# Counting the tokens of the last two batches on VectorE instead of TensorE in an attention and mixture-of-experts kernel

## The chip, the cores and the metric

The kernel runs on one core of a Trainium2 chip. The metric is the device time of one execution in microseconds. Five instruction engines work side by side: PE (TensorE, matrix products), ACT (ScalarE), DVE (VectorE), POOL (GpSimd) and SP (SyncE, which here only issues DMA transfers and loads registers). Each engine runs its own instructions in a fixed order, and semaphores tie the engines together.

## The reference

```python
# attention: u, v are (8, 2496, 256), z is (8, 2496, 64)
scores = (1 / S) * z @ z.T                 # per batch
attn   = maximum(scores, 0) ** 2           # no softmax
x      = u * (attn @ v)                    # 19968 tokens of 256
# mixture of experts: 8 experts, hidden width 1024, one expert for each token
logits = x @ w_gate + modality_bias[modality_id]
e_idx  = argmax(logits); gate = softmax(logits)[e_idx]
for e in range(8):                         # tokens of expert e
    out[mask] = gate * (maximum(x[mask] @ w1[e], 0) @ w2[e])
```

## The kernel before, in words

The first phase is attention, batch after batch. A batch is cut into five column chunks `c` of 512 queries (the last has 448), and a chunk into steps `i` of two key blocks of 128. A step makes scores `s` on PE, the root and the square on ACT (`r`), splits the square into a high part `ah` (L514, ACT mostly) and a low part `al` (L523, DVE), and PE adds three products (`ah` by `vh`, `ah` by `vl`, `al` by `vh`, L550) into four PSUM banks `acc`. Since the scores are symmetric, many squares are not computed again: DVE transposes them (`turn`, L413, L466), SP stores them in DRAM (`squares`, `corner`) and loads them for a later step (L402, L450).

When a chunk ends, ACT and DVE empty the banks into `x`, DVE multiplies by `ut` (L618), PE makes the logits (`pg`), and the chunk goes through DRAM (`rows`) into rows of one token. Then routing: `route_logits`, `route_exp`, `route_places` find the expert of each token and a running count within a partition; the counts over partitions and over earlier batches have to be added before each token's place in its expert's list is known (`route_slots`); `route_gates` makes the weight; `scatter` copies the two side columns into `x` (L802, DVE) and POOL scatters the rows into the experts' lists `xs` (L804). The kernel routes whole batches 0 to B-2; of the last batch, B-1, the first 8 columns (`SOON`) are routed before the phase ends, and the other 12 (`LATE`) within the second phase.

How the counts are added over partitions differs. For batches up to B-3, `route_sums` does it on DVE: four 32x32 transposes into `sums`, one scan over 128 values for each expert into `place`, four transposes back into `at`, one copy; at b == B-3 the total is spread over all partitions as `base` (one copy, four transposes). For the last two batches, `route_count` does it on PE: products with a triangular matrix `below` and a matrix `ones` into a bank `pc` (L746), and DVE adds them to `base` (L774, L776).

The second phase is the experts' network in tiles of 512 tokens. `choose` picks the expert with the most tokens; its first four tiles (t = -4 to -1, called EARLY) begin before the last tokens are routed. `plan` then lays out the rest; it is cut into eight parts, set between up-slices. A tile is eight up-slices (`up`: `ph` on PE, `hh` on ACT L1571, `hl` on DVE L1572) and two wide down-products (L1609). `put(slot, ...)` hangs other work behind an up-slice; slots 0 to 31 are the 32 up-slices of the tiles -4 to -1. `fetch_weights(t)` has SP load the expert's weights (`wr`, four transfers of 512 KB, L1018) after a register load from `meta`, the plan's result; ACT and DVE split them into `w` (L1033, L1038). `xg` are the tile's rows (L988), transposed into `xt` (L1065) and split into `xh`, `xl` (L1072, L1077). A tile's result goes over DRAM (`results`, L1625) back as `back` (L1628), is scaled by ACT (L1639) and scattered by POOL (L1648).

The order on every engine is written out by a planner for the first phase (a list of pieces, each with a time at which it is due) and by the order of the code for the second. Besides the diff's functions, the names that matter are `rest`, the planner's list of calls, and `between`, which `put` fills.

Of the kernel before, what the change touches and what calls it, by code (L numbers as in the profile page):

```python
# [8 lines left out]
F32 = mybir.dt.float32  # L9
F32R = mybir.dt.float32r  # L10
# [16 lines left out]
def tile_attention_moe(ctx: ExitStack, tc: tile.TileContext, ut, v, zt, mid, wg, mb, w1, w2, out):  # L27
# [71 lines left out]
    def bank_tile(shape, name):  # L99
        tag = bank["tag"]  # L100
        if isinstance(tag, list):
            tag.append(tag.pop(0))
            tag = tag[-1]
        return bank["pool"].tile(shape, F32, tag=tag, name=name)
# [9 lines left out]
    def iota_f32(shape, pattern, base, mult, name, pool=small):  # L114
        n = math.prod(shape[1:])
        i = raw.tile([P, n], I32, tag=name + "_i", name=name + "_i")
        f = pool.tile(shape, F32, name=name)
        nc.gpsimd.iota(i, pattern=pattern, base=base, channel_multiplier=mult)
        late.append((f, i))
        return f  # L120

    col = iota_f32([P, P], [[1, P]], 0, 0, "col", raw)
    part = iota_f32([P, 1], [[1, 1]], 0, 1, "part")
    em8 = iota_f32([P, E], [[1, E]], -E, 0, "em8")
    base0 = iota_f32([P, E], [[CAP, E]], -1, 0, "base0")
    begins = iota_f32([P, 1], [[0, 1]], -1, CAP, "begins")
    row_of = iota_f32([P, J], [[P, J]], 0, 1, "row_of")
    number = iota_f32([P, MAXT], [[1, MAXT]], -1, 0, "number")
    below = small.tile([P, P], F32R, name="below")
    ones = small.tile([P, P], F32R, name="ones")  # L130
    counts = small.tile([P, BLK], F32, name="counts")
    nc.vector.memset(counts, 0.0)
    sums = small.tile([BLK, P], F32, name="sums")
# [16 lines left out]
    def prep_constants(n):  # L150
        if n < 2:
            for f, i in late[n * 4:n * 4 + 4]:
                nc.vector.tensor_copy(out=f, in_=i)
            return
        nc.vector.tensor_scalar(out=below, in0=col, scalar1=part, scalar2=None, op0=ALU.is_gt)
        nc.vector.tensor_scalar(out=ones, in0=col, scalar1=0.0, scalar2=None, op0=ALU.is_ge)
        nc.vector.tensor_copy(out=place[0:E, 0:1], in_=begins[0:E])


# [549 lines left out]
    def route_places(b, cols):  # L709
        sh = RT[b]["sh"]  # L710
        shape = [P, cols.stop - cols.start, E]
        val = small.tile([P, NCOL, E], F32, tag="run", name="val")[:, 0:shape[1], :]
        em = em8.rearrange("p (o e) -> p o e", o=1).broadcast_to(shape)
        nc.vector.scalar_tensor_tensor(out=val, in0=sh, scalar=0.0, in1=em, op0=ALU.is_equal, op1=ALU.mult)
        idx = small.tile([P, NCOL, 1], F32, tag="idx", name="idx")[:, 0:shape[1], :]
        nc.vector.tensor_reduce(out=idx, in_=val, axis=AX.X, op=ALU.min)
        hot = small.tile([P, E, NCOL], F32, tag="hot", name="hot")
        if shape[1] < NCOL:
            nc.vector.memset(hot, 0.0)
        nc.vector.tensor_tensor(  # L720
            out=hot[:, :, cols].rearrange("p e j -> p j e"), in0=idx.broadcast_to(shape), in1=em, op=ALU.is_equal
        )
        if cols.stop == NCOL:
            nc.vector.memset(hot[LOW:P, :, NCOL - 2:NCOL], 0.0)
        run = small.tile([P, E, NCOL], F32, tag="run", name="run")
        nc.vector.tensor_tensor_scan(
            out=run.rearrange("p e j -> p (e j)"),
            data0=reset.rearrange("p e j -> p (e j)"),
            data1=hot.rearrange("p e j -> p (e j)"),
            initial=0.0,  # L730
            op0=ALU.mult,
            op1=ALU.add,
        )
        cnt = counts[:, 0:E] if b < B - 2 else small.tile([P, E], F32R, tag="cnt", name="cnt")
        nc.vector.tensor_copy(out=cnt, in_=run[:, :, NCOL - 1])
        RT[b].update(hot=hot, run=run, cnt=cnt)

    def route_count(b, cols):
        if b < B - 2:
            return  # L740
        cnt = RT[b]["cnt"]
        rows_of = (slice(0, P),) if cols == LATE else halves
        RT[b]["pt"] = [bank_tile([P, 2, E], "pc") for _ in rows_of]
        for n, lhs in enumerate((below, ones)):
            for pt, h in zip(RT[b]["pt"], rows_of):
                nc.tensor.matmul(out=pt[:, n, :], lhsT=lhs[h, :], rhs=cnt[h, :], start=True, stop=True)  # L746

    blocks = [slice(k * BLK, (k + 1) * BLK) for k in range(P // BLK)]

    def route_sums(b, at):  # L750

        for k in blocks:
            nc.vector.transpose(out=sums[:, k], in_=counts[k])
        nc.vector.tensor_tensor_scan(
            out=place[0:E, 1:P + 1], data0=ones[0:E].bitcast(F32), data1=sums[0:E], initial=place[0:E, 0:1],
            op0=ALU.mult, op1=ALU.add,
        )
        for k in blocks:
            nc.vector.transpose(out=at[k, :, 0], in_=place[:, k])
        nc.vector.tensor_copy(out=place[0:E, 0:1], in_=place[0:E, P:P + 1])  # L760
        if b == B - 3:
            nc.vector.tensor_copy(out=total[0:E], in_=place[0:E, 0:1].broadcast_to([E, BLK]))
            for k in blocks:
                nc.vector.transpose(out=base[k], in_=total)

    def route_slots(b, cols):
        run, hot = (RT[b][k] for k in ("run", "hot"))
        at = small.tile([P, BLK, 1], F32, tag="at", name="at")
        now = base[:, 0:E]
        if b < B - 2:  # L770
            route_sums(b, at)
        else:
            for n, x in enumerate(RT[b]["pt"]):
                nc.vector.tensor_tensor(out=at[:, 0:E, 0], in0=x[:, 0, :], in1=at[:, 0:E, 0] if n else now, op=ALU.add)  # L774
            for x in RT[b]["pt"]:
                nc.vector.tensor_tensor(out=now, in0=x[:, 1, :], in1=now, op=ALU.add)  # L776
        nc.vector.tensor_tensor(out=run, in0=run, in1=at[:, 0:E].broadcast_to([P, E, NCOL]), op=ALU.add)
        nc.vector.tensor_tensor(out=run, in0=run, in1=hot, op=ALU.mult)
        slot = small.tile([P, NCOL, 1], F32, tag="slot", name="slot")
        nc.vector.tensor_reduce(out=slot, in_=run.rearrange("p e j -> p j e"), axis=AX.X, op=ALU.add)  # L780
        sloti = small.tile([P, NCOL], I32, tag="sloti", bufs=2, name="sloti")
        nc.vector.tensor_copy(out=sloti, in_=slot[:, :, 0])
        RT[b]["sloti"] = sloti
# [36 lines left out]
    def t8(name, *shape, dt=F32):  # L820

        return small.tile([P, *(shape or (E,))], dt, name=name)
# [2 lines left out]

    def choose():

        cnt = t8("c_cnt")
        nc.vector.tensor_tensor(out=cnt, in0=base[:, 0:E], in1=base0, op=ALU.subtract)
        one_of = t8("c_most", 4)  # L830
        most, who, at = one_of[:, 0:1], one_of[:, 1:2], one_of[:, 2:4]
        nc.vector.tensor_reduce(out=most, in_=cnt, axis=AX.X, op=ALU.max)
        val = t8("c_val")
        nc.vector.scalar_tensor_tensor(out=val, in0=cnt, scalar=most, in1=em8, op0=ALU.is_equal, op1=ALU.mult)
        nc.vector.tensor_reduce(out=who, in_=val, axis=AX.X, op=ALU.min)
        nc.vector.tensor_scalar(out=skip, in0=em8, scalar1=who, scalar2=float(EARLY * T), op0=ALU.is_equal, op1=ALU.mult)
        nc.vector.tensor_scalar(out=at[:, 0:1], in0=who, scalar1=float(E), scalar2=None, op0=ALU.add)
        nc.vector.tensor_scalar(out=at[:, 1:2], in0=at[:, 0:1], scalar1=float(CAP), scalar2=None, op0=ALU.mult)
        nc.vector.tensor_copy(out=first, in_=at[0:1])

    def plan():

        cnt = t8("p_cnt")
        nc.vector.tensor_tensor(out=cnt, in0=base[:, 0:E], in1=base0, op=ALU.subtract)
        nc.vector.tensor_tensor(out=cnt, in0=cnt, in1=skip, op=ALU.subtract)

        up, upi = t8("p_up", 3, E), t8("p_upi", 3, E, dt=I32)
# [9 lines left out]
        quarters, halves, tiles = (up[:, n] for n in range(3))  # L857
        yield
        end = t8("p_end")
        nc.vector.tensor_tensor_scan(out=end, data0=ones[:, 0:E].bitcast(F32), data1=tiles, initial=0.0, op0=ALU.mult, op1=ALU.add)  # L860
        of_expert = t8("p_of", 2, E)
        beg, fin = of_expert[:, 0], of_expert[:, 1]
        start = t8("p_start")
# [564 lines left out]
    with tc.manual_schedule(engines={ET.PE, ET.Activation, ET.DVE, ET.Pool, ET.SP}):  # L1428
# [109 lines left out]
        for n, g in enumerate((24, 27, 30)):  # L1538
            at = rest.index((low, g)) + 1
            rest[at:at] = [(prep_constants, n)]  # L1540
        for f, *args in opening + rest:
            f(*args)
        for h in reversed(range(KD)):
# [294 lines left out]
    put(4, lambda: turn_rows(*end, 0))  # L1838
    put(5, lambda: turn_rows(*end, 1), lambda: store_rows(*end), lambda: load_natural(*end), lambda: make_gates(end[0], (end,)))
    put(6, lambda: take_gates(end[0], (end,)))  # L1840
    for slot, pieces in ((8, (route_gates,)), (10, (route_count, route_slots))):
        put(slot, *(lambda p=p: p(B - 1, LATE) for p in pieces))
    for n, k in enumerate(range(LATE.start, NCOL)):
        put(10 + n * 5 // 6, lambda k=k: scatter(B - 1, k))
    planning = plan()
    for slot in (10,11,12,13,14,14,15,15):
        put(slot, lambda: next(planning, None))
    put(16, lambda: fetch_weights(0))
    put(20, lambda: prefetch(-1))

    ph2.enter_context(tc.manual_schedule(engines={ET.PE, ET.Activation, ET.DVE, ET.Pool, ET.SP}))
# [117 lines left out]
```

## Time and profile before

| what | value |
|---|---|
| three runs | 2080.91, 2082.29 (median), 2083.0 us |
| profiled execution | 2084.35 us, of which the span of the program's instructions is 2082.5 us |
| PE busy | 2072.2 us, all but 10.3 us of the span |
| DVE busy | 1575.8 us (76%) |
| ACT busy | 1329.9 us (64%) |
| POOL busy | 350.1 us (17%) |
| chain that ended last | PE 95%, DMA 2%, DVE 1% |
| granted TensorE clock | 0.9 or more in all 40 slices |

Busy means that the engine executes; the span begins with the first instruction and ends with the last. A row of the timeline gives the start in us from the span's beginning, the duration, the engine, the line of the kernel, and the tile that is written and those that are read; in brackets at its end stands the idle time of the engine just before, with what ended it. The first phase ends at about 1222 us.

### The profile page before, as it was taken

What the parts mean: (1) busy time and instruction counts of PE and PEld (TensorE: products, weight loads), DVE (VectorE), ACT (ScalarE), POOL (GpSimd) and SP (SyncE); (2) the same over time, 40 slices, a digit from 0 to 9 for tenths busy, and PEclk for the clock granted to TensorE, in tenths of its full rate; (3) what the DMA queues carried; (4) which work ended last, traced back from release to release, by engine and by line L of the source; (5) the groups of instructions that cost most, each with busy time, mean ns of one, the idle gap of its engine ahead of it and who ended that gap; (6) DMA issues with size and microseconds to landing.
All of it is one profiled execution on the core that took longest, in us unless ns stands there. A gap on an engine that the chain in (4) does not pass through costs nothing.

```text
span 2082.5 us, 42408 instructions
## 1 busy us (share of the span) xinstructions
PE 2072.2 (100%) x15276; PEld 1751.1 (84%) x15276; DVE 1575.8 (76%) x2489; ACT 1329.9 (64%) x1715; POOL 350.1 (17%) x344
## 2 busy tenths in 40 slices
PE   9999999999999999999999999999999999999998
PEld 7888888889898888888888888888888888888887
DVE  9979788888888887897898776666566666666665
ACT  8659768768678678688677643545545555545554
POOL 0000022031030021030041303111211112121122
PEclk9999999999999999999999999999999999999999
DMA  8988899999889988999989976777777777776764
GB/s 202 300 265 206 252 257 236 259 255 237 257 239 242 270 238 233 279 238 240 279 240 245 271 162 181 201 187 192 202 189 197 191 196 201 183 210 186 196 187 128
DMA packets 617165, 464.82 MB, mean 223 GB/s; under 512 B 335177, under 2 KB 544105, under 8 KB 616945
## 3 DMA queue, kind: packets, MB, share of 16 engines
q1 hardware_dynamic: 601744, 420.95, 75.6%
q0 software_dynamic: 15200, 41.07, 5.7%
q8 instruction: 121, 1.98, 0.4%
q14 instruction: 100, 0.81, 0.1%
HBM read 286.27 MB, written 175.63 MB: 222 GB/s over the span
## 4 chain that ended last, share of the span: by engine, by line
PE 95%; DMA 2%; DVE 1%; SPq 1%; issue 1%; ACT 0%; POOLq 0%; ACTq 0%; POOL 0%; another core or an unknown queue 0%; DVEq 0%
PE acc L550 46%; PE ph L1567 20%; PE pw L1609 20%; PE s L375 7%; PE pg L651 1%; DMA xs<-x,sloti 0%; DVE al L523 0%; DMA r<-corner 0%; DMA vr<-in_v_dram 0%; PE po L1585 0%; DMA wr<-in_moe_w_dram 0%; DMA r<-squares 0%; DMA squares<-turn 0%; SPq L635 0%; SPq L425 0%
## 5 line engine op out<-in xcount | busy, mean ns | idle before, releaser
L550 PE MATMUL acc<-ah,vh 64*128 64x512 f32 (+1 forms) x3120 | 448.9, 383 | 0.8 <-ACT ah L514 0.5
L523 DVE TENSOR_TENSOR al<-r,ah 128x1024 fp32r<-128x1024 f32 (+1 forms) x359 | 419.6, 1183 | 31.0 <-ACT ah L514 25.1
L550 PE MATMUL acc<-al,vh 64*128 64x512 f32 (+1 forms) x3120 | 438.8, 381 | 0.0
L550 PE MATMUL acc<-ah,vl 64*128 64x512 f32 (+1 forms) x3120 | 437.1, 381 | 0.0
L1572 DVE SCALAR_TENSOR_TENSOR hl<-ph,hh 128x512 fp32r<-128x512 f32 (+1 forms) x312 | 210.3, 686 | 282.6 <-ACT hh L1571 237.3
L1567 PE MATMUL ph<-xh,w 128*128 128x512 f32 (+1 forms) x1248 | 396.0, 388 | 0.6 <-ACT xh L1072 0.6
L514 ACT CAST ah<-r 128x1024 fp32r<-128x1024 f32 (+1 forms) x342 | 345.6, 1032 | 44.6 <-PE acc L550 27.9
L804 POOL DMA_INDIRECT xs<-x,sloti x160 | 192.0, 1200 | 955.2 <-DVE x L802 689.7
L550 PEld LDWEIGHTS acc<-ah,vh 64*128 64x128 f32 x3120 | 305.0, 184 | 53.3 <-issue 1.2
L550 PEld LDWEIGHTS acc<-al,vh 64*128 64x128 f32 x3120 | 308.5, 184 | 47.9
L550 PEld LDWEIGHTS acc<-ah,vl 64*128 64x128 f32 x3120 | 301.6, 184 | 49.6
L1571 ACT ACTIVATE hh<-ph 128x512 fp32r<-128x512 f32 (+1 forms) x312 | 180.0, 592 | 235.2 <-PE ph L1567 221.9
L394 ACT ACTIVATE r<-s 128x1024 f32<-128x1024 f32 (+2 forms) x205 | 207.9, 1015 | 167.0 <-PE s L375 159.6
L1609 PE MATMUL pw<-hh,w 128*128 128x512 f32 (+1 forms) x1216 | 286.7, 388 | 0.0
L1567 PEld LDWEIGHTS ph<-xh,w 128*128 128x128 f32 x1248 | 234.2, 188 | 48.2 <-ACT xh L1072 0.9
L1609 PEld LDWEIGHTS pw<-hh,w 128*128 128x128 f32 x1216 | 228.3, 188 | 46.2
L413 DVE STREAM_TRANSPOSE turn<-r 128x512 f32<-128x512 f32 x316 | 205.3, 689 | 70.5 <-ACT r L491 44.3
L1648 POOL DMA_INDIRECT out_dram<-back,ids x152 | 148.4, 977 | 649.4 <-ACT back L1639 623.8
L1567 PE MATMUL ph<-xl,w 128*128 128x512 f32 (+1 forms) x624 | 242.2, 388 | 0.8 <-DVE xl L1077 0.8
L491 ACT ACTIVATE r<-r 128x1024 f32<-128x1024 f32 (+2 forms) x204 | 215.1, 1057 | 4.9
L375 PE MATMUL s<-zm,zk 64*128 64x512 f32 (+3 forms) x1440 | 192.5, 368 | 0.0
L1038 DVE TENSOR_TENSOR w<-wr,w 128x1024 fp32r<-128x1024 f32 x148 | 174.7, 1221 | 8.6 <-ACT w L1033 8.6
(194 smaller groups left out, 1703.0 us busy)
## 6 DMA issues: line engine op xcount, KB each, us to landing
wr<-in_moe_w_dram SPq DMA_DIRECT2D x148, 512.0 KB
squares<-turn SPq DMA_DIRECT2D x570, 128.0 KB
r<-squares SPq DMA_DIRECT2D x96, 512.0 KB
r<-squares SPq DMA_DIRECT2D x62, 448.0 KB
ut<-in_ut_dram SPq DMA_DIRECT2D x40, 512.0 KB
rows<-turn SPq DMA_DIRECT2D x160, 128.0 KB
x<-rows SPq DMA_DIRECT2D x160, 128.0 KB
xg<-xs SPq DMA_DIRECT2D x152, 128.0 KB
```

The costliest lines, as they stand in the source:

```text
L375: nc.tensor.matmul(out=s[t][:, :n_of], lhsT=lhs, rhs=mv[halves[t], ql, q], start=n == 0, stop=n == 2)
L394: nc.scalar.activation(out=r[:, t, :w], in_=s[t][:, :w] if g < 2 else s[:, :, :w], func=AF.Relu, scale=INV)
L413: nc.vector.transpose(out=dst[:, n], in_=src[:, n])
L491: nc.scalar.square(out=a[:, t, :w], in_=r[:, t, :w])
L514: copy(out=split_out(g, ah), in_=split_view(g, st_a[g]))
L523: nc.vector.tensor_tensor(out=split_out(g, al), in0=split_view(g, a), in1=split_out(g, ah).bitcast(F32), op=ALU.subtract)
L550: nc.tensor.matmul(out=acc[b, c][r][dh][:, :w], lhsT=V[b, k // J][y][halves[r], k % J, dh * P:(dh + 1) * P], rhs=x[halves[r], k % 2, :w], ...
L804: nc.gpsimd.indirect_dma_start(out=xs, out_offset=bass.IndirectOffsetOnAxis(ap=RT[b]["sloti"][:n, k:k + 1], axis=0), in_=x[:n, j, :], in_o ...
L1567: nc.tensor.matmul(out=ph, lhsT=lhs, rhs=rhs[:, k, :], start=n == 0, stop=n == 3 * KD - 1)
L1571: nc.scalar.activation(out=hh, in_=ph, func=AF.Relu)
L1572: nc.vector.scalar_tensor_tensor(out=hl, in0=ph, scalar=0.0, in1=hh.bitcast(F32), op0=ALU.max, op1=ALU.subtract)
L1609: nc.tensor.matmul(out=PO[t][h], lhsT=w[:, f, q, h * P:(h + 1) * P], rhs=HID[t, f][part], start=f == 0 and not q and not part, stop=bool(p ...
```

## The change

All batches are counted on DVE. The matrices `below`, `col` and `part` go, and so do the products into `pc`; `ones` becomes a plain constant that POOL sets. `route_sums` serves every batch, and `route_slots` calls it, but for the last 12 columns, where it stands alone in an earlier slot. The total is no longer spread once for the batches up to B-3; `all_counts` does this in `choose` and once more in `plan`. In the planner's list, three calls move: `choose` to just before `route_logits` of the first columns of the last batch, `route_slots` of the last two batches to just before their `route_gates`. In the second phase `route_sums` joins slot 8, the plan's eight parts move from slots 10, 11, 12, 13, 14, 14, 15, 15 to 11, 12, 13, 14, 14, 15, 19, 20, and the loading of tile 0's weights moves from slot 16 to slot 20.

```diff
-    below = small.tile([P, P], F32R, name="below")
-    ones = small.tile([P, P], F32R, name="ones")
+    ones = small.tile([P, P], F32, name="ones")
+    nc.gpsimd.memset(ones, 1.0)
...
-    def route_count(b, cols):
-        if b < B - 2:
-            return
-        cnt = RT[b]["cnt"]
-        rows_of = (slice(0, P),) if cols == LATE else halves
-        RT[b]["pt"] = [bank_tile([P, 2, E], "pc") for _ in rows_of]
-        for n, lhs in enumerate((below, ones)):
-            for pt, h in zip(RT[b]["pt"], rows_of):
-                nc.tensor.matmul(out=pt[:, n, :], lhsT=lhs[h, :], rhs=cnt[h, :], start=True, stop=True)
...
-        if b == B - 3:
-            nc.vector.tensor_copy(out=total[0:E], in_=place[0:E, 0:1].broadcast_to([E, BLK]))
-            for k in blocks:
-                nc.vector.transpose(out=base[k], in_=total)
+
+    def all_counts(name):
+        nc.vector.tensor_copy(out=total[0:E], in_=place[0:E, 0:1].broadcast_to([E, BLK]))
+        for k in blocks:
+            nc.vector.transpose(out=base[k], in_=total)
+        cnt = t8(name)
+        nc.vector.tensor_tensor(out=cnt, in0=base[:, 0:E], in1=base0, op=ALU.subtract)
+        return cnt
...
     def route_slots(b, cols):
-        run, hot = (RT[b][k] for k in ("run", "hot"))
-        at = small.tile([P, BLK, 1], F32, tag="at", name="at")
-        now = base[:, 0:E]
-        if b < B - 2:
-            route_sums(b, at)
-        else:
-            for n, x in enumerate(RT[b]["pt"]):
-                nc.vector.tensor_tensor(out=at[:, 0:E, 0], in0=x[:, 0, :], in1=at[:, 0:E, 0] if n else now, op=ALU.add)
-            for x in RT[b]["pt"]:
-                nc.vector.tensor_tensor(out=now, in0=x[:, 1, :], in1=now, op=ALU.add)
+        if cols != LATE:
+            route_sums(b, cols)
+        run, hot, at = (RT[b][k] for k in ("run", "hot", "at"))
...
+        for x, y in (((route_slots, B - 1, SOON), (route_gates, B - 1, SOON)), ((route_slots, B - 2, WHOLE), (route_gates, B - 2, WHOLE)), ((choose,), (route_logits, B - 1, SOON))):
+            rest.remove(x)
+            rest.insert(rest.index(y), x)
...
-    for slot, pieces in ((8, (route_gates,)), (10, (route_count, route_slots))):
+    for slot, pieces in ((8, (route_gates, route_sums)), (10, (route_slots,))):
...
-    for slot in (10,11,12,13,14,14,15,15):
+    for slot in (11,12,13,14,14,15,19,20):
         put(slot, lambda: next(planning, None))
-    put(16, lambda: fetch_weights(0))
+    put(20, lambda: fetch_weights(0))
```

On PE, the count of batch B-2 stood between two half steps of the attention; `pc` is its bank, `below` and `ones` the two matrices. Before:

```order
1680 L550 MATMUL acc<-al,vh 128x512 x4
1681 L746 MATMUL pc<-cnt,below 128x8 x2
1682 L746 MATMUL pc<-cnt,ones 128x8 x2
1683 L550 MATMUL acc<-ah,vh 128x512 x4
1684 L550 MATMUL acc<-ah,vl 128x512 x4
```

The same place now:

```order
1674 L546 MATMUL acc<-ah,vh 128x512 x4
1675 L546 MATMUL acc<-ah,vl 128x512 x4
1676 L546 MATMUL acc<-al,vh 128x512 x4
1677 L371 MATMUL s<-zm,zk 128x512 x6
1678 L546 MATMUL acc<-ah,vh 128x512 x4
1679 L546 MATMUL acc<-ah,vl 128x512 x4
1680 L546 MATMUL acc<-al,vh 128x512 x4
1681 L546 MATMUL acc<-ah,vh 128x512 x4
1682 L546 MATMUL acc<-ah,vl 128x512 x4
```

The four small products are gone, and nothing else of PE's order has moved; the other two places (four products in batch B-1, two in the second phase) are alike.

On DVE, the end of the routing of the last batch's first columns, between the low parts `al` that PE needs. Before:

```order
1266 L523 TENSOR_TENSOR al<-r,ah 128x1024
1267 L413 STREAM_TRANSPOSE turn<-r 128x2x8x32 x2
1268 L774 TENSOR_TENSOR at<-pc,base 128x8
1269 L774 TENSOR_TENSOR at<-pc,at 128x8
1270 L776 TENSOR_TENSOR base<-pc,base 128x8 x2
1271 L777 TENSOR_TENSOR run<-run,at 128x160
1272 L778 TENSOR_TENSOR run<-run,hot 128x160
1273 L780 TENSOR_REDUCE slot<-run 128x20
1274 L782 CAST sloti<-slot 128x20
1275 L802 COPY x<-side 128x2
1276 L466 STREAM_TRANSPOSE turn<-r 128x2x4x32 x2
1277 L523 TENSOR_TENSOR al<-r,ah 128x1024 x2
```

The same place now:

```order
1264 L409 STREAM_TRANSPOSE turn<-r 128x2x8x32 x2
1265 L789 COPY x<-side 128x2
1266 L462 STREAM_TRANSPOSE turn<-r 128x2x4x32 x2
1267 L519 TENSOR_TENSOR al<-r,ah 128x1024 x2
1268 L789 COPY x<-side 128x2
1269 L743 STREAM_TRANSPOSE sums<-counts 32x32 x4
1270 L744 SCALAR_TENSOR_TENSOR place<-ones,place,sums 8x128
1271 L749 STREAM_TRANSPOSE at<-place 32x32 x4
1272 L750 COPY place<-place 8x1
1273 L764 TENSOR_TENSOR run<-run,at 128x160
1274 L765 TENSOR_TENSOR run<-run,hot 128x160
1275 L767 TENSOR_REDUCE slot<-run 128x20
```

The places of the tokens now come behind the corner's transpose and two `al`, and they take ten small instructions more, less the four from `pc`. The choice of the first expert, with its five instructions of `all_counts`, stands further up, before the logits of these columns.

On SP, tile 0's weights (`wr`) in the second phase; `meta` is the plan's result, `results_113` and `results_111` belong to the tiles -4 and -3. Before:

```order
705 L1625 DMA results_113<-yt 32x16x64 x4
706 L1628 DMA back<-results_113 128x4x256
707 L1005 TENSOR_LOAD meta
708 L1005 ISA x2
709 L1018 ISA
710 L1018 DMA wr<-in_moe_w_dram 128x1024
```

The same place now:

```order
705 L1613 DMA results_113<-yt 32x16x64 x4
706 L1616 DMA back<-results_113 128x4x256
707 L1613 DMA results_111<-yt 32x16x64 x4
708 L1616 DMA back<-results_111 128x4x256
709 L990 TENSOR_LOAD meta
710 L990 ISA x2
711 L1003 ISA
712 L1003 DMA wr<-in_moe_w_dram 128x1024
```

The weights' four transfers now stand behind the next tile's results and their way back. Earlier on SP, the first register load from `first` moves from between two loads of `corner` and `squares` in batch B-1 to behind 20 more transfers.

## Rows read from the trace of the kernel before

**Rows 1.** The page: busy us of the engines, share, instructions.

```profile
PE 2072.2 (100%) x15276; PEld 1751.1 (84%) x15276; DVE 1575.8 (76%) x2489; ACT 1329.9 (64%) x1715; POOL 350.1 (17%) x344
```

**Rows 2.** Waits of PE: line, releaser, us in total, times, longest.

```profile
PE ph L1567 <- DVE xl L1077: 0.8, 1, 0.8
PE ph L1567 <- ACT xh L1072: 0.6, 1, 0.6
PE acc L550 <- ACT ah L514: 0.5, 1, 0.5
```

**Rows 3.** Windows: stretch, its us, busy us (instructions) of PE, PEld, DVE, ACT, POOL.

```profile
1224.00:2000.00 776.00, 776.00 (x3455) 645.35 (x3454) 499.01 (x731) 382.05 (x596) 144.52 (x149) 1.00 0.73 192
```

**Rows 4.** Timeline of PE around the first `pc`.

```profile
1106.71 0.61 PE L550 MATMUL acc<-al,vh 64*128 64x512 f32 x4
1107.16 0.17 PE L746 MATMUL pc<-cnt,below 64*128 64x8 f32 x2
...
1108.77 0.86 PE L375 MATMUL s<-zm,zk 64*128 64x512 f32 x6
```

**Rows 5.** Timeline of PE around the second `pc`.

```profile
1160.39 0.17 PE L746 MATMUL pc<-cnt,below 64*128 64x8 f32 x2
...
1163.38 0.62 PE L550 MATMUL acc<-ah,vh 64*128 64x512 f32 x4
```

**Rows 6.** Timeline of PE around the third `pc`, in the second phase.

```profile
1244.53 0.39 PE L1567 MATMUL ph<-xh,w 128*128 128x512 f32 x1
...
1245.20 0.39 PE L1567 MATMUL ph<-xl,w 128*128 128x512 f32 x1
```

**Rows 7.** By tile `place`: instructions, ns min/median/max, first and last start, forms.

```profile
L759 DVE STREAM_TRANSPOSE at<-place x24: 199/202/206, 273.9 to 1024.5; 32x32 f32<-32x32 f32 x24
L754 DVE TENSOR_TENSOR_SCAN place<-ones,place,sums x6: 472/473/474, 273.4 to 1023.4; 8x128 f32<-8x128 f32 x6
```

**Rows 8.** By tile `base`, columns as in rows 7.

```profile
L776 DVE TENSOR_TENSOR base<-pc,base x5: 156/166/167, 1109.3 to 1249.3; 128x8 f32<-128x8 f32 x5
```

**Rows 9.** Timeline of DVE: the choice of the first expert, and a later idle time.

```profile
1118.79 0.12 DVE L829 TENSOR_TENSOR c_cnt<-base,base 128x8 f32<-128x8 f32 x1
...
1120.29 0.17 DVE L802 COPY x<-side 128x2 f32<-128x2 f32 x1
...
1137.56 0.69 DVE L611 TENSOR_TENSOR x<-acc,x 128x512 f32<-128x512 f32 x1 [2.23 <-ACT x L607]
```

**Rows 10.** Timeline of DVE from the last batch's first places on.

```profile
1163.26 0.12 DVE L774 TENSOR_TENSOR at<-pc,base 128x8 f32<-128x8 f32 x1
...
1165.12 0.16 DVE L802 COPY x<-side 128x2 f32<-128x2 f32 x1
...
1165.94 2.32 DVE L523 TENSOR_TENSOR al<-r,ah 128x1024 fp32r<-128x1024 f32 x2
...
1186.84 1.23 DVE L523 TENSOR_TENSOR al<-r,ah 128x1024 fp32r<-128x1024 f32 x1 [9.32 <-ACT ah L514]
```

**Rows 11.** Timeline of PE: a reader of these `al`; tile 0's first product.

```profile
1167.68 0.62 PE L550 MATMUL acc<-al,vh 64*128 64x512 f32 x4
...
1306.28 0.39 PE L1567 MATMUL ph<-xh,w 128*128 128x512 f32 x1
```

**Rows 12.** Chain of waits: start us, us, what; the last corner's way back.

```profile
1179.00 6.67 DMA r<-corner
```

**Rows 13.** By tile `first`, columns as in rows 7.

```profile
L975 SPq TENSOR_LOAD <-first x4: 267/370/492, 1145.1 to 1238.6; - x4
```

**Rows 14.** Timeline of SP, tile 0's weights and what follows.

```profile
1270.95 7.14 SPq L1018 DMA_DIRECT2D wr<-in_moe_w_dram  x4
...
1284.95 0.38 SPq L1628 DMA_DIRECT2D back<-results  x1
1286.25 1.92 SPq L988 DMA_DIRECT2D xg<-xs  x4
```

**Rows 15.** Timeline of DVE where tile 0's rows are transposed.

```profile
1299.56 1.24 DVE L1065 STREAM_TRANSPOSE xt<-xg 128x1024 f32<-128x1024 f32 x1
```

More of the change, by code (lines that the diff above doesn't have):

```diff
@@ L120, in iota_f32 @@
         return f
-    col = iota_f32([P, P], [[1, P]], 0, 0, "col", raw)
-    part = iota_f32([P, 1], [[1, 1]], 0, 1, "part")
     em8 = iota_f32([P, E], [[1, E]], -E, 0, "em8")
@@ L154, in prep_constants @@
             return
-        nc.vector.tensor_scalar(out=below, in0=col, scalar1=part, scalar2=None, op0=ALU.is_gt)
-        nc.vector.tensor_scalar(out=ones, in0=col, scalar1=0.0, scalar2=None, op0=ALU.is_ge)
         nc.vector.tensor_copy(out=place[0:E, 0:1], in_=begins[0:E])
@@ L733, in route_places, with route_count, route_sums @@
         )
-        cnt = counts[:, 0:E] if b < B - 2 else small.tile([P, E], F32R, tag="cnt", name="cnt")
-        nc.vector.tensor_copy(out=cnt, in_=run[:, :, NCOL - 1])
-        RT[b].update(hot=hot, run=run, cnt=cnt)
-    def route_count(b, cols):
-        if b < B - 2:
-            return
-        cnt = RT[b]["cnt"]
-        rows_of = (slice(0, P),) if cols == LATE else halves
-        RT[b]["pt"] = [bank_tile([P, 2, E], "pc") for _ in rows_of]
-        for n, lhs in enumerate((below, ones)):
-            for pt, h in zip(RT[b]["pt"], rows_of):
-                nc.tensor.matmul(out=pt[:, n, :], lhsT=lhs[h, :], rhs=cnt[h, :], start=True, stop=True)
+        nc.vector.tensor_copy(out=counts[:, 0:E], in_=run[:, :, NCOL - 1])
+        RT[b].update(hot=hot, run=run)
     blocks = [slice(k * BLK, (k + 1) * BLK) for k in range(P // BLK)]
-    def route_sums(b, at):
+    def route_count(*_):
+        return
+    def route_sums(b, cols):
+        at = RT[b]["at"] = small.tile([P, BLK, 1], F32, tag="at", name="at")
         for k in blocks:
@@ L754, in route_sums @@
         nc.vector.tensor_tensor_scan(
-            out=place[0:E, 1:P + 1], data0=ones[0:E].bitcast(F32), data1=sums[0:E], initial=place[0:E, 0:1],
+            out=place[0:E, 1:P + 1], data0=ones[0:E], data1=sums[0:E], initial=place[0:E, 0:1],
             op0=ALU.mult, op1=ALU.add,
@@ L826, in choose @@
     def choose():
-        cnt = t8("c_cnt")
-        nc.vector.tensor_tensor(out=cnt, in0=base[:, 0:E], in1=base0, op=ALU.subtract)
+        cnt = all_counts("c_cnt")
         one_of = t8("c_most", 4)
@@ L841, in plan @@
     def plan():
-        cnt = t8("p_cnt")
-        nc.vector.tensor_tensor(out=cnt, in0=base[:, 0:E], in1=base0, op=ALU.subtract)
+        cnt = all_counts("p_cnt")
         nc.vector.tensor_tensor(out=cnt, in0=cnt, in1=skip, op=ALU.subtract)
@@ L859, in plan @@
         end = t8("p_end")
-        nc.vector.tensor_tensor_scan(out=end, data0=ones[:, 0:E].bitcast(F32), data1=tiles, initial=0.0, op0=ALU.mult, op1=ALU.add)
+        nc.vector.tensor_tensor_scan(out=end, data0=ones[:, 0:E], data1=tiles, initial=0.0, op0=ALU.mult, op1=ALU.add)
         of_expert = t8("p_of", 2, E)
```

## The prediction

> **What bounds the kernel now.** I read the page's busy times first, then the waits of TensorE (PE), then windows, then the timelines at the places that the change touches. PE is busy 2072.2 us [rows 1] of a span of 2082.5 us, so all other engines together can hold back only 10.3 us. The waits of PE name what little of it lies inside: 0.8 and 0.6 us before the first up-products of the second phase, and once 0.5 us on an `ah` [rows 2]. From 1224 to 2000 us PE is busy 776.00 of 776.00 us [rows 3]. So a gain can come only from work taken off PE or from these waits, and a loss only from a delay that outlasts the slack of an engine that is not the bound. The reader is to see that DVE's and SP's work is free as long as PE finds its operands.
>
> The sum is made against the profiled execution, 2084.35 us, which stands 2.06 us above the median of the three runs, 2082.29 us. A last step brings it back to that median.
>
> **Part 1, taken off PE.** Ten small products with their weight loads go. At the first place PE needs 1.61 us from 1107.16 to 1108.77 for three groups of four products; a group takes 0.45 us, from 1106.71 to 1107.16 [rows 4]. Three would be 1.36 us, so the four `pc` products cost 0.25 us, far less than their durations added up, since they overlap with their neighbours. At the second place it is 2.99 us for six such groups, 1160.39 to 1163.38 [rows 5], against 2.72 us: 0.27 us. At the third there are 0.67 us between a first and a third up-product [rows 6]; two products over all 128 rows take what four over 64 rows take, 0.45 us, so 0.22 us goes. Sum on PE: 0.25 + 0.27 + 0.22 = 0.74 us, or 0.04% of the time. That is the most that the change takes directly.
>
> Not all is kept. The first two places lie ahead of the wait on `ah`. That wait does not follow PE: DVE stood idle 9.32 us for the same `ah` at 1186.84 [rows 10], and the chain of waits there runs over the last corner's way back from DRAM, 6.67 us from 1179.00 [rows 12]. If PE arrives 0.52 us sooner and the corner does not, PE waits 0.52 us longer. The second wait, at the phase change, ends a chain that goes on from there over scatters on POOL, another corner and the first weights; it does not follow PE either. The third place lies in the gapless stretch, and its 0.22 us stays.
>
> **Part 2, added to DVE.** One call of the sums is eight transposes at 0.20 us, a scan at 0.47 us [rows 7] and a copy; for this and the other small copies I take the 0.17 us of an add of eight elements [rows 8]. That makes 1.6 + 0.47 + 0.17 = 2.2 us. It comes three times, and replaces four, four and two small adds, about 0.17 us each. The total and `base` in `choose` and `plan` are a copy and four transposes, about 1.0 us each; one such group was there before, in batch B-3.
>
> In batch B-2 the sums and slots (3.6 us with the four operations on `run`) now stand directly before the gates. `choose`, 1.50 us from 1118.79 to 1120.29 [rows 9], goes away from there. Net, what follows is about 2.1 us late. DVE has idle time to take it up, 2.23 us in one piece at 1137.56 alone [rows 9]. In between every `al` could be late; PE would wait 2.1 us at the very most. I take nothing, since PE has no wait on an `al` anywhere in the list of before [rows 2], so DVE is ahead here by some amount.
>
> In the first columns of B-1, `choose` with its `base`, 1.50 + 1.0 = 2.5 us, comes in first; the slots, 1.86 us from 1163.26 to 1165.12 [rows 10], go behind two `al`. So the corner's transpose and these two `al` are 0.7 us late. The first of them, half of the 2.32 us from 1165.94, was ready at 1167.1 [rows 10], and PE reads it at 1167.68 [rows 11]. It would be ready at 1167.8, while PE, 0.5 us ahead, asks at 1167.2: PE waits about 0.6 us here, between 0 and 1. That eats the gain of the first two places, which is lost at the corner anyway. The sums and slots behind them make the rest up to 4.3 us late, against an idle time of 9.32 us on DVE [rows 10]. All of it fits, so nothing of this reaches the second phase unless the corner moves.
>
> In the second phase the sums (2.2 us) and the plan's `base` are in slots 8 to 11, in which DVE is about 2 us later with `hl`. The bank that a slot needs is that of four slots earlier, and the order leaves this distance as it was. I take nothing, at most 1 us.
>
> **Part 3, SP's order.** The register load from `first`, 0.27 to 0.49 us each [rows 13], leaves the stretch before the last corner, with its two register instructions perhaps 0.9 us. Everything on SP behind it could be that much sooner, the corner that ends PE's wait included; against that stands the corner's transpose, 0.7 us later on DVE, and a load of `ut` that waits for DVE's product, later by 4.3 us, ahead of the corner's load. Ends: 0.9 us sooner, 0.6 us later. I take 0.1 us sooner, since SP was issuing into full queues and a place freed there is not a transfer made faster.
>
> **Part 4, tile 0's weights.** Before, their four issues ran from 1270.95 for 7.14 us, and the rows `xg` were issued from 1286.25 [rows 14]. Now the weights follow a `back` which was issued at 1284.95 [rows 14]: weights from about 1285.4 to 1292.5, `xg` from about 1292.6 on, 6.3 us later than before, for 1.92 us [rows 14]. If the last of it takes as long as the corner, 6.67 us [rows 12], it lands at 1301.2; before it was used from 1299.56 [rows 15], and three steps of about 1.24 us (transpose, high, low) would end at 1304.9. PE's first product of tile 0 started at 1306.28 [rows 11]. It fits, with 1.4 us to spare. I take nothing; the other end is 3 us, if weights and rows queue behind each other for twice the corner's time or so.
>
> This is 2.5 MB within 10 us, hence a question of transfers. SBUF tiles on the left side now start 576 bytes lower. The Trainium skill ("DMA: Bandwidth & Descriptors", "How a descriptor splits into AXI transactions") says that a descriptor which does not start on a 256-byte boundary costs one more, partly unused transaction; for bulk tiles that start on such a boundary now and did not before, this would make transfers slightly cheaper, for token rows nothing. No row shows a transfer's alignment, and by rows 2 PE waits for DMA hardly at all, so by the rule as by the rows the sum stays.
>
> **Sum.** 2084.35 - 0.22 (third place) - 0.1 (corner) = 2084.0 us profiled, and less 2.06 us: 2082.0 us against the median of before. Within 0.2%, or 4.2 us, a measurement of this kernel cannot tell a change; the forecast is no change.
>
> **Rivals.**
> The first: everything is kept. SP's freed 0.9 us moves the corner and the chain behind it, so both waits shrink with PE's earlier arrival: -0.74 - 0.9 = -1.6 us, 2080.7 us. For it: the chain runs through SP several times [rows 12]. Against: `ut` and the transpose are later.
>
> The second is slower: tile 0's weights and rows come late, PE waits before its first up-product of tile 0, and nothing later gives it back, since PE is the bound. It decides from a landing of `xg` after about 1302.6 (1306.28 less three steps of 1.24 us). At a landing of 1306, nearly 5 us behind the slow landing above, the price is 3.4 us less the 0.3 gained: 2085.4 us. For it: 2 MB ahead of the rows in the same queues, and a `back` before them that had to wait for its results. Against: the four weights' issues took only 7.14 us with other transfers beside them [rows 14].
>
> The third: late low parts on DVE make PE wait where I take nothing: 2.1 us in batch B-2 and up to 1 us in the second phase. A wait ahead of the corner is taken back there up to 0.5 us, so +1.6 + 1 - 0.3: 2084.6 us at its worst.
>
> The fourth: the change doesn't do what it says: PE's small products were hidden in its pipeline, and leaving them out gives nothing: 2082.3 us, not to be told from the forecast.
>
> **How the numbers follow.** Forecast 0.66; rival 1 0.12; rival 2 0.10; rival 3 0.08; rival 4 0.04. The range reaches from below rival 1 to rival 2's price, 2079.8 to 2085.4 us, with a microsecond for the spread of the runs of before (2.1 us). Faster by over 0.2% needs 4.2 us, more than PE's work and all its inner waits (0.74 + 1.9 us) can give: 0.04. Slower by over 0.2% needs rival 2 at more than its price, or 2 and 3 together: 0.08. Same: 0.88.
>
> **What would show it.** Right: PE busy about 0.7 us less, no `pc`; PE's wait on `ah` near 1186 longer by about what is saved ahead of it; the rows of `xt` for tile 0 still ending before PE asks. Wrong: a wait of PE on `xl`, `xh` or `w` at about 1306 us; a wait on `al` over 1 us between 1110 and 1180; a phase change more than a microsecond earlier or later than before; a new wait on a `ph` bank between 1245 and 1280.

## The result and the profile after

The change made the kernel slower, by 13 us: 2094.77 us (median of 6, 2093.68 to 2096.96) against 2081.74 us (median of 6), a ratio of 1.0064 with a 95% interval of 1.0055 to 1.0074. The forecast was 2082.0 us, no change, and its range ended at 2085.4.

The page of the changed kernel, busy us as in [rows 1]:

```profile
PE 2083.7 (100%) x15266; PEld 1759.2 (84%) x15266; DVE 1583.8 (76%) x2510; ACT 1331.8 (64%) x1715; POOL 351.2 (17%) x343
```

PE executes ten products less and is busy 11.5 us more. The waits of PE, as in [rows 2]:

```profile
PE warm L1417 <- POOL zeros L110: 1.0, 1, 1.0
PE acc L546 <- DVE ah L494: 0.6, 1, 0.6
PE acc L546 <- DVE al L519: 0.5, 1, 0.5
```

The reader is to see what is not there: no wait in the second phase, none at the phase change. PE is not held back by anybody; it works more slowly. The stretch of [rows 3], after:

```profile
1224.00:2000.00 776.00, 776.00 (x3397) 635.18 (x3396) 497.07 (x733) 377.67 (x586) 145.08 (x148) 1.00 0.66 189
```

In the same 776 us, at the same granted clock of 1.00 (the 2.4 GHz level), PE starts 3397 products where it started 3455. (The last three numbers of such a row are the granted clock, the busy share of the DMA engines and the GB/s that they moved.) The timeline shows it product by product. Before, the first up-products of a tile:

```profile
1458.60 0.39 PE L1567 MATMUL ph<-xh,w 128*128 128x512 f32 x1
...
1459.73 0.61 PE L1567 MATMUL ph<-xh,w 128*128 128x512 f32 x2
```

After, the same five products of a tile that reads the weights W_0 (the tiles take W_0 and W_1 in turn):

```profile
1459.52 0.40 PE L1555 MATMUL ph<-xh,w 128*128 128x512 f32 x1
...
1460.69 0.63 PE L1555 MATMUL ph<-xh,w 128*128 128x512 f32 x2
```

And further on in a tile that reads W_1, three products:

```profile
1450.45 0.62 PE L1555 MATMUL ph<-xh,w 128*128 128x512 f32 x2
...
1451.13 0.62 PE L1555 MATMUL ph<-xh,w 128*128 128x512 f32 x2
```

From start to start that is 1.13 us for five before, 0.227 us each; 1.17 us, 0.234 each, with W_0; and 0.68 us for three, again 0.227, with W_1. From the starts of the products in the trace, 96 products (a tile's work) took 21.76 us before, in tile after tile. After, the tiles -4 to -1, which all read W_0, took 22.40 us, and later tiles 22.00 and 22.24 in turn. Over the 39 stretches of 96 products (`pc` left out of the count) it sums up to 855.9 us against 843.1, or 12.8 us, which is nearly all of the 13.0 lost. The 843.1 us hold the two waits of [rows 2] at the phase change, 0.8 and 0.6 us, which the changed kernel didn't have; the pace alone costs a little more, as e3 below shows.

What has W_0 to do with the change? Nothing reads or writes it differently, but tiles lie elsewhere. `below` (512 bytes a partition), `part` and `cnt` (32 each) are gone from the left side of SBUF, and every tile stacked behind them starts 576 bytes lower: `xh`, `xl`, `hh`, `hl`, W_1, and the attention's `vh`, `vl`, `ah`, `al`. 576 is 2 x 256 + 64. Before, all of these started 64 bytes past a multiple of 256; now they start at one. W_0 lies on the right side, in a pool opened after the constants' pool is closed. It stayed, 64 bytes past. These places are worked out from the program, for no trace shows an address; the experiments below test them. So weights and moving operand of one product lie alike (modulo 256) with W_1 and no longer with W_0.

### The profile page after: what moved, and what is told of

It reads as the page before. It is cut to its first block, busy times and chain, and to the rows that moved or that the text cites. A ratio compares the mean times of both kernels' runs of the same rounds, so it can differ in the third digit from the quotient of the medians.

```text
span 2092.9 us, 42408 instructions
## 1 busy us (share of the span) xinstructions
PE 2083.7 (100%) x15266; PEld 1759.2 (84%) x15266; DVE 1583.8 (76%) x2510; ACT 1331.8 (64%) x1715; POOL 351.2 (17%) x343
## 4 chain that ended last, share of the span: by engine, by line
PE 98%; issue 1%; ACT 0%; DMA 0%; DVE 0%; SPq 0%; POOLq 0%; POOL 0%; another core or an unknown queue 0%; DVEq 0%
PE acc L546 49%; PE ph L1555 21%; PE pw L1597 20%; PE s L371 7%; PE pg L647 1%; DMA squares<-turn 0%; PE warm L1417 0%; PE ph L1703 0%; ACT w L1018 0%; ACT r L390 0%; ACT back L1627 0%; DVE y L1674 0%; ACT part L1669 0%; SPq L421 0%; POOLq L1953 0%
## 5 line engine op out<-in xcount | busy, mean ns | idle before, releaser
L1555 PE MATMUL ph<-xh,w 128*128 128x512 f32 (+1 forms) x1248 | 400.5, 392 | 0.0
L1597 PE MATMUL pw<-hh,w 128*128 128x512 f32 (+1 forms) x1216 | 291.4, 392 | 0.0
```

Source lines behind the costliest of these rows:

```text
L1555: nc.tensor.matmul(out=ph, lhsT=lhs, rhs=rhs[:, k, :], start=n == 0, stop=n == 3 * KD - 1)
L1597: nc.tensor.matmul(out=PO[t][h], lhsT=w[:, f, q, h * P:(h + 1) * P], rhs=HID[t, f][part], start=f == 0 and not q and not part, stop=bool(p ...
```

## The experiments

The experiments move tiles by changing the size of unused tiles called `room`, of which the kernel has four; the second number of each diff line is in floats of 4 bytes. They ran in four groups on different chips, each beside the kernel before, whose own time there was 2079.27, 2080.68, 2081.59 and 2082.54 us; so times are compared within a group. Rows are the stretch from 1400 to 2000 us, columns as in [rows 3]: what counts is the number of products behind PE's 600.00 us. For the first two kernels it is, before and after:

```profile
1400.00:2000.00 600.00, 600.00 (x2666) 500.03 (x2665) 381.40 (x503) 304.88 (x472) 105.27 (x109) 1.00 0.73 194
```
```profile
1400.00:2000.00 600.00, 600.00 (x2625) 492.75 (x2624) 379.31 (x498) 302.07 (x464) 105.22 (x108) 1.00 0.66 190
```

**e1_after_left64**, the changed kernel with the left side where it was:

```diff
-    small.tile([P, 16], F32, name="room")
+    small.tile([P, 160], F32, name="room")
```

> The changed kernel with an unused tile made 576 bytes larger, so that every tile on the left side of SBUF (xh, xl, hh, hl, the weights W_1 of odd-even turn, and the attention's tiles) begins where it did before the change, 64 bytes past a multiple of 256, as the weights W_0 on the right side do in both kernels. Nothing else differs from the changed kernel. Theory A (places: PE's products in the second phase slow down when weights and moving operand begin at different offsets within 256 bytes): every up- and down-product is back at 0.227 us, a tile at 21.76 us instead of 22.00 and 22.24, PE busy about 2071 us, and as the phase change stays 3.4 us earlier than before, the time is 2078.5 to 2080 us. Rival B (order: the later work on DVE and SP slows PE): stays at 2094 to 2096 us.

Measured: 2079.90 us against 2079.27 (ratio 1.0007, 0.9998 to 1.0016).

```profile
1400.00:2000.00 600.00, 600.00 (x2666) 500.03 (x2665) 381.30 (x505) 306.14 (x474) 107.43 (x111) 1.00 0.72 195
```

The loss is gone with all of the change in order and counting left in. The gain of 3 us that I read from the phase change isn't there: see e9 and the next section.

**e2_before_left0**, the kernel before with its left side 64 bytes lower and nothing else:

```diff
-    small.tile([P, 16], F32, name="room")
```

> The kernel before with its first unused tile of 64 bytes left out, so that all tiles on the left side begin 64 bytes lower, at multiples of 256, while W_0 on the right side stays 64 past one; the order on every engine is that of the kernel before. Theory A: the products that read W_0 slow down, tiles -4 to -1 take about 22.4 us and of the others every second half-weighted 22.00 and 22.24 us, in all about 39 tiles x 0.36 = +13 us, 2095 to 2096 us. Rival B: unchanged, 2082 us.

Measured: 2092.61 us against 2079.27 (1.0065, 1.0049 to 1.0080); tiles of 22.40, then 22.00 and 22.24 us.

```profile
1400.00:2000.00 600.00, 600.00 (x2625) 492.75 (x2624) 378.96 (x498) 301.98 (x465) 104.97 (x108) 1.00 0.67 190
```

The whole loss without any of the change. Rival B, the order, is out.

**e3_after_w0at0**, the changed kernel with W_0 moved to a multiple of 256 too (W_0 is on the right side, where a larger `room` puts it lower):

```diff
-        pool.tile([P, 40], F32, name="room")
+        pool.tile([P, 56], F32, name="room")
```

> The changed kernel with an unused tile above W_0 64 bytes larger, so that W_0 on the right side too begins at a multiple of 256, as all on the left side does after the change. Theory A (weights and moving operand must lie alike, whatever the common offset): 21.76 us a tile, 2078.5 to 2080 us. Theory A' (the offset 64 itself is the good one): W_0's products stay slow or all get slow, 2094 us or more. Rival B: 2094 us.

Measured: 2078.36 us against 2079.27 (0.9997, 0.9988 to 1.0007), every full tile 21.76 us.

```profile
1400.00:2000.00 600.00, 600.00 (x2665) 499.87 (x2664) 379.88 (x502) 305.56 (x472) 109.15 (x112) 1.00 0.67 195
```

It is not the offset 64 that is good, but that weights and moving operand share one. The 39 stretches of 96 products take 841.7 us here; the changed kernel, with the same order and, like e3, no wait in the second phase, took 855.9, so the pace alone costs 14.2 us.

**e4_before_w0at0**, the same edit made to the kernel before, so that W_0 is at 0 and the left side at 64:

> The kernel before with W_0 at a multiple of 256 and everything on the left 64 past one: the difference of the changed kernel, with its sign turned. Theory A with a difference that counts either way: products with W_0 slow, about 2095 us. If only a moving operand below the weights' offset costs: 2082 us. Rival B: 2082 us.

Measured: 2082.16 us (one run; before 2079.27).

```profile
1400.00:2000.00 600.00, 600.00 (x2652) 497.79 (x2652) 378.56 (x500) 303.96 (x469) 106.19 (x109) 1.00 0.70 193
```

Neither expectation holds: tiles -3 and -2 take 21.97 us, 0.21 over 21.76 and so a third of what such a tile loses in e2. The difference counts both ways, but not equally.

**e5_after_w0at128, e6_after_w0at192, e11_after_w0at32**: the changed kernel (left side at 0) with the `room` of e3, 40 floats, made 24, 8 and 48, which puts W_0 at 128, 192 and 32. The first of the three:

```diff
-        pool.tile([P, 40], F32, name="room")
+        pool.tile([P, 24], F32, name="room")
```

> The changed kernel with W_0 begun at 128 past a multiple of 256 (64 in the changed kernel) by a smaller unused tile above it; all on the left at 0. If the loss is one of any difference between weights and moving operand: tiles -4 to -1, which read W_0 alone, at about 22.4 us again. If it goes with the size of the difference or lies in 64-byte pieces: another number between 21.76 and 24 us. If only the difference of 64 costs: 21.76 us.

> The same with W_0 at 192. If what counts is the difference weights minus moving operand modulo 256, this is the -64 of the earlier run with W_0 at 0 and the left side at 64: tiles -4 to -1 at 21.97 us, the others 21.83 and 21.90. If the common offset counts too, another number.

> The changed kernel with W_0 begun at 32 past a multiple of 256, all on the left at 0. With W_0 at 64, 128 and 192 two tiles together took 44.24, 44.14 and 43.73 us, with W_0 at 0 43.52 us. If the loss comes by whole pieces of 64 bytes that weights and moving operand share: 43.52 us, as at 0. If any difference costs: 43.7 us or more.

Measured: 2092.05 and 2084.32 us (before 2080.68), and 2093.27 us (before 2082.54), one run each. The rows, in that order:

```profile
1400.00:2000.00 600.00, 600.00 (x2630) 494.26 (x2629) 379.11 (x499) 302.07 (x464) 105.05 (x108) 1.00 0.66 191
```
```profile
1400.00:2000.00 600.00, 600.00 (x2652) 497.68 (x2651) 378.53 (x500) 304.22 (x469) 106.37 (x110) 1.00 0.68 194
```
```profile
1400.00:2000.00 600.00, 600.00 (x2627) 492.87 (x2626) 379.21 (x499) 302.12 (x464) 105.23 (x108) 1.00 0.67 190
```

With weights minus moving operand at 0, 32, 64, 128 and 192 bytes past a multiple of 256, PE starts 2665, 2627, 2625, 2630 and 2652 products; tiles -3 and -2 take 22.40 us at 32, 64 and 128. e6 is e4's difference (-64 is 192 modulo 256) at other places of both, with the same tile times (21.97, then 21.83 and 21.90): by these two, the difference modulo 256 is what counts. 32 bytes cost as much as 64, so it doesn't go by shared pieces of 64 bytes.

**e7_after_x0_h64**, the changed kernel with `hh`, `hl` and W_1 moved up to 64, where W_0 lies, and `xh`, `xl` left at 0:

```diff
-    rows.tile([P, 24], F32, name="room")
+    rows.tile([P, 40], F32, name="room")
```

> The changed kernel with an unused tile behind the x ring's pool start 64 bytes larger: xh and xl stay at 0, while hh, hl and W_1 go to 64, where W_0 lies. Theory A (weights against the moving operand of the same product): all up-products are slow in every tile and all down-products run at 0.227 us, so every tile takes about 21.76 + 0.32 = 22.1 us, and two tiles in turn no longer differ. If the place of the weights against each other counts: 21.76 us. If hh and hl against xh and xl counts: both halves slow.

Measured: 2100.89 us (one run; before 2080.68), every full tile of the steady stretch 22.12 us. Timeline of PE, from 24 up-products over 24 down-products to the next up-products:

```profile
1420.84 0.39 PE L1555 MATMUL ph<-xh,w 128*128 128x512 f32 x1
...
1426.44 3.81 PE L1597 MATMUL pw<-hh,w 128*128 128x512 f32 x16
1430.09 1.98 PE L1597 MATMUL pw<-hl,w 128*128 128x512 f32 x8
1431.90 0.39 PE L1555 MATMUL ph<-xh,w 128*128 128x512 f32 x1
```

24 up-products take 5.60 us, 0.233 each; 24 down-products 5.46 us, 0.227 but for the first few. The same weights are slow against one moving operand and fast against another, so it is the pair. The time is 6 us more than I worked out from the tiles; about as much is lost in the attention, spread evenly over it (0.5 us in 100). There the scores' operands were left at 0 with `xh`, and `vh`, `ah` moved to 64, so the two operands of each product `s` and `acc` still begin alike, but products of both offsets follow each other. That neighbours disturb each other too is a reading of this one run; it wasn't tried alone.

**e8_v64_ah0**, e1 with the attention's `ah`, `al` moved against `vh`, `vl`:

```diff
             V[0, 0] = tuple(bulk.tile([P, J, D], F32R, tag=n, bufs=6, name=n) for n in ("vh", "vl"))
+            bulk.tile([P, 48], F32, name="gap")
```

> The changed kernel with its left side restored to 64, and in the attention an unused tile of 192 bytes between the vh, vl tiles (at 64) and the ah, al tiles (then at 0). The second phase is untouched. Theory A as a property of every product: the attention's products, two at a time over 64 rows, slow down by the 6.6 ns that W_0's products lost, 9360 / 2 x 6.6 ns = 31 us, 2110 us. If it belongs to products over all 128 rows or to the second phase alone: 2080 us.

Measured: 2105.99 us (one run; before 2080.68), full tiles of the second phase at 21.76 us. Timelines of PE in the attention, first e1, then e8:

```profile
401.45 1.07 PE L546 MATMUL acc<-ah,vh 64*128 64x512 f32 x8
402.36 1.07 PE L546 MATMUL acc<-ah,vl 64*128 64x512 f32 x8
```
```profile
401.18 1.09 PE L547 MATMUL acc<-ah,vl 64*128 64x512 f32 x8
402.12 1.09 PE L547 MATMUL acc<-al,vh 64*128 64x512 f32 x8
```

Eight products, two at a time, start 0.91 us apart in e1 and 0.94 in e8. It is no matter of the second phase or of products over all rows. The cost came out at some 25 us instead of 31.

**e9_left64_slots**, e1 with the second phase's slots as before the change:

```diff
-    for slot in (11,12,13,14,14,15,19,20):
+    for slot in (10,11,12,13,14,14,15,15):
...
-    put(20, lambda: fetch_weights(0))
+    put(16, lambda: fetch_weights(0))
```

> The changed kernel with its left side restored to 64, and in the second phase the plan's parts back in slots 10 to 15 and the loading of tile 0's weights back in slot 16; the rest of the change stays. The first such run, with the slots as changed, had one wait of PE of 1.7 us beside tile 1's first up-products, behind a `back` issued at 1306.5 us. If the later weights cause it: `back` about 7 us earlier, no wait of PE in the second phase, tile 0 at 21.76 us, the time 0.9992 of before, 0.7 us faster. If it is chance: a wait of 0 to 2 us remains.

Measured: 2082.86 us against 2081.59 (1.0006, 0.9997 to 1.0015), no gain over e1. PE's waits in the second phase, first e1's, then e9's:

```profile
1317.34 0.50 PE L1555 MATMUL ph<-xh,w 128*128 128x512 f32 x1 [1.03 <-DVE hl L1560]
```
```profile
1252.49 0.50 PE L1555 MATMUL ph<-xh,w 128*128 128x512 f32 x1 [0.44 <-DVE hl L1560]
1278.54 1.99 PE L1597 MATMUL pw<-hh,w 128*128 128x512 f32 x8 [0.31 <-issue]
```

The wait of e1 is gone (it stood in the second half of tile 0, 15 us after its first product at 1302.15 us, not at tile 1 as I had written; of the 1.7 us lost, 1.03 are the wait of the row). But the counting and the plan, close together again, delay DVE's `hl` and the tiles before: in e1 one stretch of 96 products took 23.49 us, 1.73 over 21.76; in e9 two took 22.54 and 22.71, together 1.73 over. Between these two profiles the moved slots exchange one delay for the other; my expectation missed the second half of that. The first delay doesn't always come with the moved slots: e3, of e1's order, has 21.76 us in every full tile, with its `back` issued at 1304.04 instead of 1306.46 us, while e8, with the left side at 64 like e1, waits 1.0 us at the same place. e1 and e3 differ in the common offset alone, and their medians by 1.5 us (2079.90 and 2078.36); whether the offset makes `back` late enough for this delay is open.

**e10_before_all0**, the kernel before with the left side and W_0 both at multiples of 256 (the edits of e2 and e3):

> The kernel before with everything at multiples of 256, left side and W_0 alike. Theory A: 21.76 us in every tile, the time of before, 1.000 within 0.001. If multiples of 256 are better or worse than 64 past one for anything else (transfers, the other engines): another time, with all the tiles' products at 0.227 us.

Measured: 2082.30 us against 2081.59 (1.0004, 0.9995 to 1.0013).

```profile
1400.00:2000.00 600.00, 600.00 (x2666) 500.02 (x2665) 380.08 (x503) 305.92 (x472) 108.08 (x111) 1.00 0.67 195
```

With the order of before, the common offset costs no time that these runs could tell. The DMA engines do show it: their busy share in this stretch is 0.67 here and in e3, with the left side at multiples of 256, and 0.73 and 0.72 in the kernel before and e1, with it 64 past, at 194 to 195 GB/s in all four.

## Why the prediction was wrong

The step that failed is the first: "a loss only from a delay that outlasts the slack of an engine that is not the bound". It took the duration of PE's own products as given. I had seen the shift of 576 bytes, and weighed it for transfers only; there the sentence on the rule of the Trainium skill ended in "the sum stays". The runs put in its place a longer pace of PE's own products: +12.8 us against the profile of before, +14.2 against e3, which has the order of the changed kernel and no wait there. It lies on about 2,000 of the 3,800 products of the second phase, those of the 21 tiles that read W_0, with some 6.7 ns more each (22.40 against 21.76 us for 96).

Part 1, the ten products: right in kind, they are gone, and no run's time tells their 0.74 us from the spread. The third place can be read from the starts of the products: the second stretch of 96 takes 22.03 us in the kernel before and in e10, with `pc`, and 21.76 in e1 and e3, without, so 0.27 us against my 0.22. That the first two places' share is given back at the two waits of [rows 2] couldn't be seen: these waits belong to that execution. e2, with the order of before, has neither of them, and e3 and e10 have none at the phase change either; so PE's lead of 3.4 us there over the profile of before is no effect of the change.

Part 2, DVE's lateness: I expected about 0.6 us of waiting on the first of two `al` near 1167 us. There was none; DVE reached these `al` at 1164.39 us, sooner than in [rows 10]. A wait on an `al` of 0.5 us stands at 1135.78, in batch B-2, where DVE idled 3.40 us for the store of `squares`; I had taken nothing there and bounded it by 2.1. It came in e1 and e6 too, with 0.5 and 0.4 us, and not in the other runs with the order of the change, nor in any with that of before. So rival 3's wait is there now and then, with half a microsecond, but not by its mechanism: DVE was not busy with added work ahead of it, but idle.

Part 3: the last corner's `ah` reached DVE at 1181.46 us instead of 1186.84, far more than the 0.9 us that SP's freed load could give. As it came at 1180.99 us in e2 as well, with the order of before, and the wait was missing there too, no part of it can be put down to SP's order.

Part 4, tile 0's weights: the issue is where it was put, behind a `back`. SP, after:

```profile
1280.90 0.38 SPq L1616 DMA_DIRECT2D back<-results  x1
1282.12 2.25 SPq L1003 DMA_DIRECT2D wr<-in_moe_w_dram  x4
1285.28 2.25 SPq L973 DMA_DIRECT2D xg<-xs  x4
```

The `back` came 4 us sooner than in [rows 14] (PE was some 2 us ahead here), for it no longer stands behind the weights, and the four issues took 2.25 us instead of 7.14. So `xg` was no later than before, and in the changed kernel PE waited for nothing here. At PE's full pace, in e1, PE lost 1.7 us, but 15 us after tile 0's first product, where rival 2 had placed it, and for `hl` instead of the tile's rows; e3, at full pace too, lost nothing. What the order costs or gives in all is below what these runs resolve: 1.0007, 0.9997 and 1.0006 in e1, e3 and e9, each with 1 in its interval.

On transfers my guess had the direction right, but it bears on no time here: with the left side at multiples of 256 the DMA engines are busy 0.67 of the stretch from 1400 to 2000 us (e3 and e10), with it 64 past 0.72 and 0.73 (e1 and before), for the same GB/s. e10's time, a ratio of 1.0004, doesn't show it, as PE waits for no transfer there; which transfers became cheaper no run tells. The rule of the Trainium skill ("DMA: Bandwidth & Descriptors", "How a descriptor splits into AXI transactions") is that a descriptor which starts off a 256-byte boundary begins with a transaction that is partly unused; one transaction more, as the prediction put it, is what its example of 576 bytes shows, while its example of 96 bytes takes one either way. The busy shares agree with the rule's direction.

What stays open is why. That the load of one product's weights and the reading of another's moving operand get in each other's way would fit e7, but no run separates them. Open is also why a slow stretch lasts about six products into the next, fast one.

## What to carry to other kernels

In a kernel that TensorE bounds without gaps, compare the start-to-start time of equal products before looking for waits: a busy share of 100% on both sides hides a pace that changed by 1.5%. A tile added or removed anywhere moves all that is stacked behind it, so after any such edit see whether weights and moving operand of each product still begin alike modulo 256 bytes, and pad if not. When an edit of order gives a surprise, run the old order at the new places and the new order at the old ones first; two runs settled it here.

## What the runs showed of the hardware

A product's pace depends on where its two SBUF operands begin relative to each other: 0.227 us a product where both begin alike modulo 256 bytes, up to 0.233 us (3%) where the weights begin 32, 64 or 128 bytes further, about 0.229 us at 192 (from 21.97 us for 96). The common offset, 0 or 64, makes no difference to the pace. For pairs of products over 64 rows only 64 bytes were tried (e8): eight start 0.94 us apart instead of 0.91. In e7 the attention lost some 6 us though the operands of its products `s` and `acc` begin alike; there products of offset 0 and of offset 64 follow each other, and why that costs wasn't tried. The granted clock is 1.00 in all these stretches, so the clock's level is not what changes. Transfers use the DMA engines less when the SBUF tiles on the left side begin at multiples of 256 bytes: a busy share of 0.67 (e3, e10) instead of 0.72 and 0.73 (e1, before) at 194 to 195 GB/s.
